# Storing the last output block by quarters, with its fourth quarter summed ahead of its second

## The chip, the cores and the metric

The kernel runs on one core of one Trainium2 chip. The metric is the device time of one execution in microseconds (us). Runs shown are medians of several executions; the profile comes from one execution of its own.

## What is computed

Hash attention over 4 x 8 heads (768 positions of 64 values each), whose output goes, as 3072 rows of 512 features, through a two-matrix block with a squared ReLU. In the reference, cut:

```python
q_bucket = ...   # 6 sign bits of q @ proj, as a number; k_bucket likewise
mask = q_bucket[:, :, :, None] == k_bucket[:, :, None, :]
scores = np.where(mask, scale * np.matmul(q, k.transpose(0, 1, 3, 2)), -1000000000.0)
...
attn = attn / (np.sum(attn, axis=-1, keepdims=True) + 1e-09)
x = np.matmul(attn, v)          # brought to (3072, 512)
h = x @ w_in                    # (512, 2048)
r = np.maximum(h, 0.0)
return ((r * r) @ w_out)        # (2048, 512), fp32
```

## The kernel before

The kernel has two stages. In the first, a loop over 16 pairs of heads hashes, scores, exponentiates and multiplies by the values, and leaves the attention output, feature by feature, in DRAM. In the second, a loop over three chunks of 1024 rows (`NCHUNK` = 3, `NCH` = 1024) computes the hidden layer and then calls `project(i)` for the second matrix.

Both matrices are multiplied by a fast scheme with seven half-size products in place of eight, applied twice for the second matrix: an outer round `k` of seven, and in each round seven inner products of 128 x 128 weight tiles (`leaf`) with 256 columns. The inner seven are written out in `product` (L828), in a fixed order: each of them adds four matmuls to one of three accumulators in PSUM (`add`, L837), ScalarE keeps running sums of them (`keep`, L844: `one`, `two`, `five`, `three`), and the four callbacks `c11`, `c12`, `c22`, `c21` take the four quarters out as soon as their operands are there. `c11`, `c12`, `c21` and `c22` are the quarters 0, 1, 2 and 3 of a block of 256 features x 512 rows: quarter `n` lies in row `n // 2` (128 features) and column `n % 2` (256 rows, `QN`). The work of every engine stands in the order of these calls; nothing is reordered later (`tc.manual_schedule()`).

The outer rounds add the quarters to sums that are kept in SBUF (`add_to`, L1196). A block of the output is finished in the second, sixth and fourth of the uses; the last round (`k` = 6) of the last chunk calls `fourth` and finishes the block `(ih, jh) = (1, 0)`, the last of the kernel. There `c11`, `c12` and `c22` each make two adds on VectorE (first a temporary from PSUM or from the kept sums, then the sum `o`), and `c21` makes one.

What stands in `o` has features on the partitions and must be turned. `close` does it when both quarters of a row are there:

- `put_out` (L1207): VectorE transposes the row's 128 x 512 in blocks of 32 x 32 (L1210), and four stores write it in pieces of 128 bytes (L1217). For the last block two of the four go through GpSimd's queue (POOL), two through SyncE's (SP).
- `put_last` (L1222), for the second row of the last block only: TensorE transposes each quarter in two 128 x 128 parts (L1227), ScalarE (quarter 3, L1232) or VectorE (quarter 2, L1234) copies the 128 x 256 from PSUM, and two stores on SP (quarter 3) or ScalarE's queue (quarter 2) write pieces of 512 bytes (L1237).

The buffers `h` that take what is to be stored are five (`NH`), used in turn, and each is free when its stores have landed.

Behind the last block every engine loads the flag `slow` (L1473) and branches on it (L1474): where it is set, a general version of the whole computation would run (`general`); here it is not, and the engines jump over that code. SyncE then waits for the semaphores of the DMAs, and all engines meet at a barrier (shown as L1671).

Of the kernel before, what the change touches and what calls it, by code (L numbers as in the profile page):

```python
# [8 lines left out]
FP32 = mybir.dt.float32  # L9
# [25 lines left out]
def kernel(  # L35
# [10 lines left out]
    nc = tc.nc  # L46
# [6 lines left out]
    P = 128  # L53
# [12 lines left out]
    NCH = 1024  # L66
    NCHUNK = B * S // NCH
# [3 lines left out]
    ident = glob.tile([P, P], FP32, name="ident")  # L71
# [10 lines left out]
    HF, HD, NR, NQ = DFF // 2, DM // 2, NFF // 2, NFF // 4  # L82
# [539 lines left out]
    for pr in range(NIN, NP):  # L622
        n = 16 if pr == NP - 1 else 1 + (pr % 3 == 0)
# [4 lines left out]
    def load_x(i, fs=slice(0, NFT)):  # L628

        if i not in xs:  # L630
            x = p_c.tile([P, NFT, NCH], FP32, name="x")
            xs[i] = x, [p_c.tile([P, 2, NCH // 2], FP32, name=f"t_x{n}") for n in range(3)]
        nc.gpsimd.dma_start(out=xs[i][0][:, fs], in_=x_all[:, fs, i * NCH:(i + 1) * NCH])
# [23 lines left out]
    with tc.manual_schedule():  # L657
# [158 lines left out]
        p_r = fast.enter_context(tc.tile_pool(name="p_r", bufs=2, reuse_waits="tile"))  # L816
        p_k = fast.enter_context(tc.tile_pool(name="p_k", bufs=1, reuse_waits="tile"))
        ps_m = fast.enter_context(tc.tile_pool(name="ps_m", bufs=2, space=PSUM, reuse_waits="tile"))
        HN, QN, NH = NCH // 2, NCH // 4, 5
# [5 lines left out]

        KEPT = dict(one=2, two=1, three=2, five=1)

        def product(n, w, at, bt, c11, c12, c21, c22, hook=None):  # L828

            acc = [ps_m.tile([P, 512], FP32, name=f"acc{i}")[:, 0:w] for i in range(3)]

            def add(to, a, b, first, last):
                for i in range(n):
                    nc.tensor.matmul(  # L837
                        out=acc[to], lhsT=a(i), rhs=b(i), start=first and i == 0,
                        stop=last and i == n - 1, skip_group_check=True,
                    )  # L840

            def keep(of, name):
                t = p_r.tile([P, 512], FP32, name=name, bufs=KEPT[name])[:, 0:w]
                nc.scalar.copy(out=t, in_=acc[of])  # L844
                return t

            add(0, at(0), bt["11"], True, False)
            one = keep(0, "one")
            add(1, at(1), bt["21"], True, True)
            if hook:  # L850
                hook()
            c11(acc[1], one)
            add(0, at(4), bt["t2"], False, False)
            two = keep(0, "two")
            add(2, at(3), bt["t1"], True, False)
            five = keep(2, "five")
            add(0, at(5), bt["t3"], False, False)
            three = keep(0, "three")
            add(2, at(6), bt["22"], False, True)
            c12(acc[2], two)  # L860
            c22(three, five)
            add(0, at(2), bt["t4"], False, True)
            c21(acc[0])

# [83 lines left out]
        def factor_units(n):  # L948

            src = [new_h().rearrange("p (a f c) -> p a f c", a=2, c=P) for _ in range(2)]  # L950
            for j in range(2):
                nc.gpsimd.dma_start(out=src[j], in_=w_in_7[j * NQ + n, :, 5:7])
            sums = [new_h().rearrange("p (a f c) -> p a f c", a=2, c=P) for _ in range(2)]
            sums_a(
                src[0][:, :, 0], src[0][:, :, 1], src[1][:, :, 0], src[1][:, :, 1],
                *(sums[j // 2][:, :, j % 2] for j in range(4)),
            )
            for m in range(2):
                nc.gpsimd.dma_start(out=w_in_49[n, :, 0:2, 2 * m:2 * m + 2], in_=sums[m])
# [246 lines left out]
        def put_out(i, ih, jh, n, o):  # L1206


            ot = p_r.tile([P, HN], FP32, name="h", bufs=NH)
            nc.vector.transpose(out=ot, in_=o)  # L1210
            m0 = ih * HD + n * P
            at = slice(i * NCH + jh * HN, i * NCH + (jh + 1) * HN)
            for a in range(P // 32):
                queue = nc.gpsimd if (ih, jh) == (1, 1) else nc.sync
                if (i, ih, jh) == (NCHUNK - 1, 1, 0) and a % 2:
                    queue = nc.gpsimd
                queue.dma_start(  # L1217
                    out=out[at, m0 + a * 32:m0 + (a + 1) * 32].rearrange("(c i) j -> i c j", i=32),
                    in_=ot[a * 32:(a + 1) * 32].rearrange("i (c j) -> i c j", j=32),
                )  # L1220

        def put_last(n, o):  # L1222

            row, col = n // 2, n % 2
            tp = ps_m.tile([P, 512], FP32, name=f"acc{col}")[:, 0:QN]
            for t in range(QN // P):
                nc.tensor.transpose(  # L1227
                    out=tp[:, t * P:(t + 1) * P], in_=o[:, t * P:(t + 1) * P], identity=ident
                )
            ot = p_r.tile([P, HN], FP32, name="h", bufs=NH)[:, 0:QN]  # L1230
            if col:
                nc.scalar.copy(out=ot, in_=tp)  # L1232
            else:
                nc.vector.tensor_copy(out=ot, in_=tp)  # L1234
            lo = (NCHUNK - 1) * NCH + col * QN
            for t in range(QN // P):
                (nc.sync if col else nc.scalar).dma_start(  # L1237
                    out=out[lo + t * P:lo + (t + 1) * P, HD + row * P:HD + (row + 1) * P],
                    in_=ot[:, t * P:(t + 1) * P],
                )  # L1240

        def project(i):
# [12 lines left out]
            def close(ih, jh, n):  # L1255
                o = outs[ih, jh, n // 2]
                o[1] += 1
                if (i, ih, jh, n // 2) == (NCHUNK - 1, 1, 0, 1):

                    if o[1] == 2:  # L1260
                        for col in (1, 0):
                            put_last(n - n % 2 + col, o[0][:, col * QN:(col + 1) * QN])
                elif o[1] == 2:
                    put_out(i, ih, jh, n // 2, o[0])

# [37 lines left out]
            for k in range(7):  # L1303
                b = OUTER[k][1]
                t1, t2 = tens.pop(k)
                if k == 0 and more:
                    load_x(i + 1)
                if i == 0 and 0 < k <= NQ:
                    factor_units(k - 1)
                if i == 0 and k == NQ + 1:  # L1310
                    load_peak(0)
                    load_peak(1)
                if k >= 5 and more:
                    load_inner(i + 1, 0, (k - 5,))
                at = lambda m, k=k: lambda n: leaves[k, m][:, n]
                bt = {
                    "11": lambda n: b[:, n, 0:QN], "21": lambda n: b[:, NQ + n, 0:QN],
                    "22": lambda n: b[:, NQ + n, QN:HN], "t1": lambda n: t1[:, n],
                    "t2": lambda n: t2[:, n], "t3": lambda n: b[:, n, QN:HN],
                    "t4": lambda n: b[:, NQ + n, 0:QN],  # L1320
                }

                def hook():
                    y21 = b[:, NQ:NR, 0:QN]
                    minus(y21, y21, t2)
                    if k + 1 < 7 and k not in (1, 3):
                        inner_sums(k + 1)
                    if k == 6 and more:
                        load_third_inner(i + 1, 0, nc.scalar)
                        sums_inner(i + 1)  # L1330

                counted = []

                def a_with_load(m, k=k):
                    load_leaf(7 * k + len(counted) + NLEAF - 2)
                    counted.append(m)
                    return at(m)

                use = uses[k]
                product(  # L1340
                    NQ, QN, a_with_load, bt, lambda *p: use(0, *p), lambda *p: use(1, *p),
                    lambda p: use(2, p, None), lambda *p: use(3, *p), hook,
                )
                if k in (3, 4) and i + 1 < NCHUNK:
                    sum_x(i + 1, 2 * k - 5)
                    sum_x(i + 1, 2 * k - 4)
                if k == 5 and i + 1 == NCHUNK:
                    guard()
                if k == 0:

                    for h in range(2):
                        at_h = slice(h * NQ, (h + 1) * NQ)
                        minus(b11[:, at_h], b22[:, at_h], b_t[:, at_h])
                    inner_sums(2)
                if k == 2:

                    for h in range(2):
                        at_h = slice(h * NQ, (h + 1) * NQ)
                        minus(b_t[:, at_h], b21[:, at_h], b11[:, at_h])
                    inner_sums(4)  # L1360
# [314 lines left out]
```

## Time and profile before

| | us |
|---|---|
| median of 3 runs (861.77 to 862.26) | 862.15 |
| time of the profiled execution | 861.97 |
| its span (first to last instruction) | 859.9 |
| TensorE busy | 848.5 |
| VectorE busy | 748.7 |
| ScalarE busy | 402.1 |
| GpSimd busy | 166.8 |

TensorE's granted clock is 0.998 over the span. The profile names the engines PE (TensorE), DVE (VectorE), ACT (ScalarE), POOL (GpSimd) and SP (SyncE); "SPq" and the like are instructions on an engine's queue that count as no busy time, such as the issue of a DMA. L1196 is line 1196 of the kernel. In the timeline each row has its start, its duration, and how many instructions it stands for; in the chain of waits each row is a piece of the chain of work that ended last.

### The profile page before, as it was taken

Reading aid. Unit: us, or ns where it says so; the run is one execution under the profiler, and the core shown is the slowest. Engines: PE = TensorE matmul, PEld = TensorE weight load, DVE = VectorE, ACT = ScalarE, POOL = GpSimd, SP = SyncE. Lnnn points to the kernel's source line nnn. Section 1 sums busy time; section 2 is a strip of 40 time slices with the busy share of each in tenths; the row PEclk is TensorE's granted clock in tenths of the full one; section 3 lists DMA queues with packets and bytes.
Section 4 is the critical chain, followed back from the end, with each engine's and each line's share of the span. In section 5 each row is a group of like instructions: output and inputs, shape, how many; then the busy total and the mean of one; then the engine's idle time right before and its main releaser. Section 6 shows DMA issues by size and latency. Waiting matters only on the chain.

```text
span 859.9 us, 16991 instructions
## 1 busy us (share of the span) xinstructions
PE 848.5 (99%) x6595; PEld 527.0 (61%) x6595; DVE 748.7 (87%) x1024; ACT 402.1 (47%) x752; POOL 166.8 (19%) x280
## 2 busy tenths in 40 slices
PE   8999999999999999999999999999999999999996
PEld 3544444444444444444788866657888765678885
DVE  5899999999999988988979978888889788888875
ACT  5887777888777752222111145553111355541110
POOL 1321111123221101642122121111000211100003
PEclk9999999999999999999999999999999999999999
DMA  9676889879998516999977975538558865345465
GB/s 204 133 149 150 179 176 203 208 162 252 250 229 209 179 58 237 337 320 300 349 234 220 265 191 192 186 110 299 164 151 201 195 203 179 122 129 159 148 177 107
DMA packets 234758, 170.14 MB, mean 198 GB/s; under 512 B 167944, under 2 KB 191824, under 8 KB 234672
## 3 DMA queue, kind: packets, MB, share of 16 engines
q1 hardware_dynamic: 194944, 87.85, 40.9%
q0 software_dynamic: 16480, 42.48, 15.8%
q10 hardware_dynamic: 23248, 38.68, 14.8%
q8 instruction: 53, 0.87, 0.4%
q14 instruction: 33, 0.27, 0.1%
HBM read 127.14 MB, written 41.16 MB: 196 GB/s over the span
## 4 chain that ended last, share of the span: by engine, by line
PE 98%; DVE 1%; DMA 1%; ACT 0%; issue 0%; DVEq 0%
PE acc L837 41%; PE st L430 18%; PE xo L485 14%; PE acc L1094 13%; PE acc L1047 8%; PE tot L534 2%; PE hash L360 1%; DMA qk_nat<-in_q_dram 1%; PE tp L320 0%; DVE bits L410 0%; ACT feat L327 0%; PE xo L360 0%; DVE o L1196 0%; ACT e L436 0%; PE acc L1227 0%
## 5 line engine op out<-in xcount | busy, mean ns | idle before, releaser
L436 ACT ACTIVATE e<-st 128x768 f32<-128x768 f32 x192 | 155.4, 810 | 58.3 <-PE st L430 55.3
L430 PE MATMUL st<-feat 64*64 64x384 f32 x1536 | 157.1, 483 | 1.0 <-DVE feat L329 1.0
L485 PE MATMUL xo<-e,v_nat 64*64 64x385 f32 (+1 forms) x1520 | 156.9, 483 | 0.0
L837 PE MATMUL acc<-b,leaf 128*128 128x256 f32 x600 | 133.2, 379 | 0.3 <-issue 0.3
L837 PEld LDWEIGHTS acc<-b,leaf 128*128 128x128 f32 x600 | 113.9, 190 | 16.6 <-issue 1.2
L473 DVE TENSOR_TENSOR total<-total,e 128x1536 f32<-128x1536 f32 x64 | 111.8, 1746 | 4.3 <-ACT e L436 2.8
L396 POOL DMA_DIRECT2D bits<-signed x120 | 61.9, 520 | 217.3 <-ACT signed L385 198.5
L485 PEld LDWEIGHTS xo<-e,v_nat 64*64 64x64 f32 (+1 forms) x1520 | 55.9, 133 | 67.9 <-issue 59.1
L1094 PE MATMUL acc<-t_x,w_unit 128*128 128x512 f32 x192 | 91.0, 596 | 0.0
L430 PEld LDWEIGHTS st<-feat 64*64 64x64 f32 x1536 | 55.7, 133 | 39.1 <-issue 33.5
L837 PE MATMUL acc<-t,leaf 128*128 128x256 f32 x336 | 75.9, 379 | 0.0
L837 PEld LDWEIGHTS acc<-t,leaf 128*128 128x128 f32 x336 | 63.8, 190 | 8.7
L909 DVE SCALAR_TENSOR_TENSOR b<-h 128x512 f32<-128x512 f32 x96 | 65.7, 691 | 3.0
L430 PE MATMUL st<-bits 64*64 64x384 bf16 x768 | 64.7, 325 | 0.1
L837 PE MATMUL acc<-x,w_unit 128*128 128x512 f32 x128 | 56.5, 593 | 0.0
L837 PE MATMUL acc<-b_t,leaf 128*128 128x256 f32 x240 | 53.8, 379 | 0.0
L844 ACT COPY two<-acc 128x256 f32<-128x256 f32 (+1 forms) x29 | 12.5, 431 | 87.5 <-PE acc L837 72.1
L1217 POOL DMA_DIRECT2D out_dram<-h x26 | 16.8, 654 | 186.0 <-DVE h L1210 184.4
L1094 PEld LDWEIGHTS acc<-t_x,w_unit 128*128 128x128 f32 x192 | 35.7, 190 | 27.0 <-issue 23.0
L837 PEld LDWEIGHTS acc<-b_t,leaf 128*128 128x128 f32 x240 | 45.5, 190 | 6.3
L844 ACT COPY one<-acc 128x256 f32<-128x256 f32 (+1 forms) x29 | 12.5, 431 | 78.7 <-PE acc L837 49.2
L430 PEld LDWEIGHTS <-bits 64*64 64x64 bf16 x768 | 23.8, 106 | 38.0 <-issue 37.1
(176 smaller groups left out, 1287.8 us busy)
## 6 DMA issues: line engine op xcount, KB each, us to landing
leaf<-w_out ACTq DMA_DIRECT2D x142, 256.0 KB, 3.1
raw<-in_moe_w_in_dram SPq DMA_DIRECT2D x8, 1024.0 KB, 6.7
raw<-in_moe_w_out_dram SPq DMA_DIRECT2D x8, 1024.0 KB, 7.6
w_unit<-w_in SPq DMA_DIRECT2D x16, 512.0 KB, 4.1
w_unit<-w_in SPq DMA_DIRECT2D x8, 896.0 KB, 8.3
w_out<-sums POOLq DMA_DIRECT2D x16, 448.0 KB, 8.0
v_nat<-in_v_dram SPq DMA_DIRECT2D x16, 384.0 KB, 5.2
x_all<-x_t SPq DMA_DIRECT2D x16, 384.0 KB, 3.1
```

The source lines that it names most:

```text
L396: nc.gpsimd.dma_start(out=t[h * D:h * D + NBITS + 1, w, c * HS:(c + 1) * HS], in_=signed[at:at + NBITS + 1, h],)
L430: nc.tensor.matmul(out=st[k * HK:(k + 1) * HK, h, 0:HS], lhsT=src[1][rows, key], rhs=src[0][rows, cut], start=first, stop=not first, skip_ ...
L436: nc.scalar.activation(out=key_of(pr, kt)[:, :, i, 0:HS], in_=st[:, :, 0:HS], func=ACTF.Exp, scale=scale)
L473: nc.vector.tensor_tensor(out=totals[pr], in0=totals[pr], in1=e, op=ALU.add)
L485: return nc.tensor.matmul(out=outs[pr][h * D:(h + 1) * D, c, 0:HS + 1], lhsT=nat[pr, "v_nat"][rows, h, kt * D:(kt + 1) * D], rhs=key_of(pr ...
L534: done = nc.tensor.matmul(out=spares[pr][g * 32:(g + 1) * 32, c2, 0:QS], lhsT=ones[rows], rhs=totals[pr][rows, h, c, c2 * QS:(c2 + 1) * QS ...
L837: nc.tensor.matmul(out=acc[to], lhsT=a(i), rhs=b(i), start=first and i == 0, stop=last and i == n - 1, skip_group_check=True,)
L844: nc.scalar.copy(out=t, in_=acc[of])
L909: nc.vector.scalar_tensor_tensor(out=out, in0=h, scalar=0.0, in1=h, op0=ALU.max, op1=ALU.mult)
L1047: nc.tensor.matmul(out=out, lhsT=w(a), rhs=b, start=start, stop=stop, skip_group_check=True)
L1094: nc.tensor.matmul(out=to, lhsT=w[:, PLACE[a], f], rhs=bt[b](f), start=first and f == 0, stop=last and f == NFT // 2 - 1, skip_group_check ...
L1217: queue.dma_start(out=out[at, m0 + a * 32:m0 + (a + 1) * 32].rearrange("(c i) j -> i c j", i=32), in_=ot[a * 32:(a + 1) * 32].rearrange("i ...
```

## The change

The order of the last two callbacks but one in `product` changes for the last round of the last chunk: quarter 3, which needs only the kept sums `three` and `five`, is taken ahead of quarter 1. Each quarter of the last block is turned and stored by itself as soon as it is summed. Quarters 0, 3 and 1 go through a 128 x 256 transpose on VectorE and four stores of 128-byte pieces each (`put_part`), two on SP and two on POOL. Quarter 2, the last, goes through TensorE in two parts, of which VectorE copies the first, which SP stores, and ScalarE copies and stores the second. Before, both quarters of the second row went through TensorE, and the first row was stored as a whole. The number of products, adds and copies of sums is the same; two 128 x 128 transposes on TensorE fall away, and three 128 x 256 transposes on VectorE stand for one of 128 x 512.

```diff
-        def product(n, w, at, bt, c11, c12, c21, c22, hook=None):
+        def product(n, w, at, bt, c11, c12, c21, c22, hook=None, last=False):
...
             add(2, at(6), bt["22"], False, True)
+            if last:
+                c22(three, five)
             c12(acc[2], two)
-            c22(three, five)
+            if not last:
+                c22(three, five)
             add(0, at(2), bt["t4"], False, True)
             c21(acc[0])
...
                 queue = nc.gpsimd if (ih, jh) == (1, 1) else nc.sync
-                if (i, ih, jh) == (NCHUNK - 1, 1, 0) and a % 2:
-                    queue = nc.gpsimd
...
+        LATE = {0: (nc.gpsimd, nc.sync), 3: (nc.sync, nc.gpsimd), 1: (nc.sync, nc.gpsimd)}
+
+        def put_part(n, o):
+
+            row, col = n // 2, n % 2
+            ot = p_r.tile([P, HN], FP32, name="h", bufs=NH)[:, 0:QN]
+            nc.vector.transpose(out=ot, in_=o)
+            lo = (NCHUNK - 1) * NCH + col * QN
+            m0 = HD + row * P
+            for a in range(P // 32):
+                LATE[n][a % 2].dma_start(
+                    out=out[lo:lo + QN, m0 + a * 32:m0 + (a + 1) * 32].rearrange(
+                        "(c i) j -> i c j", i=32
+                    ),
+                    in_=ot[a * 32:(a + 1) * 32].rearrange("i (c j) -> i c j", j=32),
+                )
+
         def put_last(n, o):
 
             row, col = n // 2, n % 2
-            tp = ps_m.tile([P, 512], FP32, name=f"acc{col}")[:, 0:QN]
-            for t in range(QN // P):
-                nc.tensor.transpose(
-                    out=tp[:, t * P:(t + 1) * P], in_=o[:, t * P:(t + 1) * P], identity=ident
-                )
             ot = p_r.tile([P, HN], FP32, name="h", bufs=NH)[:, 0:QN]
-            if col:
-                nc.scalar.copy(out=ot, in_=tp)
-            else:
-                nc.vector.tensor_copy(out=ot, in_=tp)
             lo = (NCHUNK - 1) * NCH + col * QN
             for t in range(QN // P):
-                (nc.sync if col else nc.scalar).dma_start(
+                at = slice(t * P, (t + 1) * P)
+                tp = ps_m.tile([P, 512], FP32, name=f"acc{t}")[:, 0:P]
+                nc.tensor.transpose(out=tp, in_=o[:, at], identity=ident)
+                if t:
+                    nc.scalar.copy(out=ot[:, at], in_=tp)
+                else:
+                    nc.vector.tensor_copy(out=ot[:, at], in_=tp)
+                (nc.scalar if t else nc.sync).dma_start(
                     out=out[lo + t * P:lo + (t + 1) * P, HD + row * P:HD + (row + 1) * P],
-                    in_=ot[:, t * P:(t + 1) * P],
+                    in_=ot[:, at],
                 )
...
-                if (i, ih, jh, n // 2) == (NCHUNK - 1, 1, 0, 1):
-
-                    if o[1] == 2:
-                        for col in (1, 0):
-                            put_last(n - n % 2 + col, o[0][:, col * QN:(col + 1) * QN])
+                if (i, ih, jh) == (NCHUNK - 1, 1, 0):
+                    put = put_last if n == 2 else put_part
+                    put(n, o[0][:, n % 2 * QN:(n % 2 + 1) * QN])
                 elif o[1] == 2:
                     put_out(i, ih, jh, n // 2, o[0])
...
                     lambda p: use(2, p, None), lambda *p: use(3, *p), hook,
+                    (i, k) == (NCHUNK - 1, 6),
```

## The prediction

> **What bounds the kernel now.** I read the page first (busy time and chain), then the chain of waits of the last 15 us, the timeline of VectorE and SyncE there, and the rows of the lines that end the program.
>
> ```profile
> span 859.9 us, 16991 instructions
> PE 848.5 (99%) x6595; PEld 527.0 (61%) x6595; DVE 748.7 (87%) x1024; ACT 402.1 (47%) x752; POOL 166.8 (19%) x280
> PE 98%; DVE 1%; DMA 1%; ACT 0%; issue 0%; DVEq 0%
> ```
>
> TensorE sets the pace for 851 of the 860 us. Its instructions up to the end of the last product are the same before and after (the built programs differ only in the transposes behind it), so only what follows that product can change. The chain there, in order of time:
>
> ```profile
> 844.84 4.55 PE acc L837 x21
> ...
> 849.48 0.44 DVE tmp L1196
> 849.92 0.02 issue
> 849.94 0.44 DVE o L1196
> 850.38 0.02 issue
> 850.40 0.71 DVE h L1210
> 851.11 0.32 DVE tmp L1196
> 851.43 0.02 issue
> 851.46 0.44 DVE o L1196
> 851.89 0.04 issue
> 851.94 0.78 PE acc L1227 x4
> 852.72 0.02 issue
> 852.74 0.42 DVE h L1234
> ```
>
> The chain leaves TensorE at 849.39, while TensorE works on: its last product runs to 851.10 (the timeline's last group of products starts at 845.76 and takes 5.34). So VectorE, not TensorE, is late: the add that needs the last product (L1196, `o<-sum,acc`) starts at 851.80, 0.7 us after its operand. The view ends with the last busy instruction, at 853.16; the span ends 6.7 us later. For these I read SyncE's rows. In the timeline, its last two stores:
>
> ```profile
> 852.81 0.84 SPq L1237 DMA_DIRECT2D out_dram<-h  x2
> ```
>
> Among the rows of the lines that end the program, the load of the flag, the branch on it and the waits behind it (duration in ns, first and last start):
>
> ```profile
> L1473 SPq TENSOR_LOAD <-slow x1: 735/735/735, 853.7 to 853.7; - x1
> ```
> ```profile
> L1474 SPq EVENT_SEMAPHORE  x8: 17/17/17, 857.7 to 858.2; - x8
> ...
> L1474 SPq COMPARE_BRANCH  x1: 50/50/50, 854.5 to 854.5; - x1
> ```
>
> And in the queue's own waits (us in total, times, longest):
>
> ```profile
> SPq L1474 <- SPq L1474: 3.1, 1, 3.1
> ```
>
> The reader is to see SyncE alone: two stores issued until 853.65, the flag loaded from 853.70, the branch at 854.51, then 3.1 us in which SyncE waits for nothing but itself, then its waits for the DMA semaphores from 857.66 and the final barrier to 859.9. The last store landed at 857.10 (issued by ScalarE at 853.61, 3.5 us), so the first of these waits came 0.55 us after everything had landed. The other engines had passed their branches by 855.3 and stood at the barrier (GpSimd's drain, 3.4 us, ended at 856.4). **The end is SyncE's own sequence behind its last store**, and what moves that store moves the end.
>
> **The change, part by part.** Times are of the profiled execution: span 859.9, its own time 861.97, 0.18 under the median 862.15.
>
> *Quarter 0, stored alone.* Its sum ends at 846.84 (846.42 + 0.43). VectorE then idled 2.64 us until 849.48. A 128x256 transpose is not in the trace; 128x384 takes 0.58 (L547), 128x512 0.71 (L1210), so 0.13 per 128 columns, and I take 0.45 (bounds: nothing, and 0.71). It lies in the idle time: 0. Its two SP and two POOL issues find free queues (POOL's earlier stores end at 847.45): 0.
>
> *Quarter 3 ahead of quarter 1.* It needs `three`, which ScalarE has ready at 848.06 (847.69 + 0.37). Add 0.38, add 0.42, transpose 0.45, and three gaps of 0.03: ready at 849.4, just before quarter 1's operand (849.48). With the transpose at 0.71 quarter 1 would start 0.25 late, but it has that much to spare: its two adds (0.44 each with their gaps) and a transpose end at 850.85, and the last product only comes at 851.10. So all this is hidden in VectorE's wait for TensorE; if the cover were gone, the chain would again carry the 1.2 us.
>
> *Quarter 2, the last.* Before, its add stood behind one 128x512 transpose (0.71) and quarter 3's two adds. Now it starts at 851.13 (851.10 and the 0.03 that ScalarE's copies lag behind TensorE), 0.67 earlier, and ends at 851.55. Then to SyncE's flag load:
> - add to transposes: 0.05 (852.22 to 852.27 before), so 851.60;
> - the first 128x128 transpose alone: 0.33 (L1227's longest) and 0.03, so the copy starts at 851.96;
> - VectorE copies 128x128. The rows are 0.42 for 128x256 (L1234) and 0.56 for 128x384 (L329): 0.29 by their slope. Bounds 0.18 (128x24, L555) and 0.42. I take 0.29, as it lies on the line of two PSUM copies: 852.25;
> - the issue starts 0.03 later, 852.28, and takes 0.35 to 0.44 (L1237): 0.40, to 852.68. There is one issue on SyncE instead of two;
> - the flag load begins 0.06 later: 852.74, against 853.70.
>
> Sum: **0.96 us earlier**, 0.8 to 1.1 with the bounds of copy and issue.
>
> *SyncE's queue.* Six issues of 128-byte pieces now stand ahead of the last store instead of two. Quarter 3's pair starts at 849.42, quarter 1's at 850.88. L1217 issues in this stretch took 0.32 to 0.91, median 0.49, so the queue is free at about 851.9, 0.4 before the last store: 0. If every one took 0.91, see below.
>
> *The other half on ScalarE.* Its transpose ends 0.11 after the first; a 128x128 copy is 0.27 (0.37 for 128x256, 0.59 for 128x512): issue at 852.37, against 853.20 and 853.61 before. With L1237's 3.5 to 3.8 us both last stores land by 856.2.
>
> *After the branch.* Branch at 853.55, 3.1 us, waits from 856.7, by which time the last store (856.2) has landed: 0.5 in hand, as before. The semaphores waited on are as many as before. GpSimd's last issue comes 0.26 earlier (851.79 against 852.05). So the whole 0.96 arrives at the end: 861.97 - 0.96 = 861.0, and on the median 862.15 - 0.96 = **861.2**.
>
> *The 3.1 us.* The trace shows an 8 KB instruction packet (q14) at 855.70 and another at 855.86, 1.2 us behind SyncE's branch, and no other engine waited more than 0.6 us at its branch. So I read the stall as a fetch of the branch's target, with a cost that starts at the branch and moves with it. [...] After the change SyncE has five instructions more ahead of the branch and jumps as far.
>
> **The rivals.**
> 1. *The stall is not a fixed cost* (the fetch is quicker, or the wait is really for the stores). Then the landing at 856.1 to 856.2 sets the end, without the 0.55 now lost: 857.66 - 856.1 = 1.55 earlier, 860.6. If the 0.55 goes with the landing, the end follows ScalarE's last issue, 853.61 to 852.37: 1.24 earlier, 860.9. For it: the stall is the largest piece behind the last product. Against it: SyncE was released well after the landing, and nothing shortens the jump.
> 2. *SyncE's queue becomes the bound, slower than before.* With all five issues from 849.42 on (quarters 3 and 1, and the last) at 0.91, the flag load starts at 849.42 + 5 x 0.91 + 0.06 = 854.03, 0.33 later than before: 862.5. It decides against the change from a mean of (853.64 - 849.42) / 5 = 0.84 per issue. The median 0.49 speaks against it; that the longest rows stand where DMA queues are full speaks for it.
> 3. *SyncE's code crosses a fetch boundary.* Its 26 instructions behind the branch now lie five further on. If they straddle a boundary of the 8 KB packets, a second stall of up to 3.1 us stands on the path: about 865. In the trace these packets follow SyncE's instruction count at a period of 128, and by this count 7 or so are left to the boundary.
> 4. *Nothing is gained*: the DMA traffic or the barrier, not SyncE, holds the end at 859.9: 862.1. Against it: every engine but SyncE has arrived by 856.4.
>
> **How the numbers follow.** Forecast 0.72 (861.2; 860.9 to 861.5 by itself), rival 1 0.13 (860.6 to 860.9), rival 2 0.07 (up to 862.5), rival 3 0.03 (865), rival 4 0.05 (862.1). The range 860.3 to 862.2 holds the forecast, rivals 1 and 4, and part of 2. About 0.2% (1.7 us) is what a measurement of this kernel can tell from no change; to be faster by that, the time must fall below 860.4, which is the far edge of rival 1 only: 0.06. Slower by that is rival 3: 0.03. Within: 0.91.
>
> **What would show it.** In the changed profile: no VectorE idle time ahead of quarter 3's add other than for `three`; the last add starting within 0.1 us of TensorE's last product; a 128x128 copy near 0.29; one SP store at about 852.3; SyncE's flag load near 852.7; again 3.1 us at its branch, and the span at about 858.9. I am wrong if SyncE's stall changes, if the flag load is not about 1 us earlier, or if a store lands after 856.7.

## The result, and the profile after

| | before | after |
|---|---|---|
| median of 20 runs (us) | 862.40 | 860.93 |
| ratio, 95% interval | | 0.9985 (0.9978 to 0.9992) |
| span of the profiled execution | 859.9 | 859.6 |
| end of TensorE's last product, from the span's start | 851.10 | 851.70 |
| from there to the span's end ("the tail") | 8.79 | 7.88 |

By the ratio the kernel is 1.3 us faster (0.7 to 1.9), against 0.96 forecast (861.2, counted from the 862.15 of three runs). The last product ended 0.6 us later in the second profile: what lies ahead of it scatters by more than the change is worth (849.9 to 853.3 in the profiles below). So from here on times are counted from the end of the last product, and the tail is what is compared: 0.9 us shorter.

The chain of the last microseconds, where before it left TensorE at 849.39:

```profile
845.87 5.84 PE acc L837 x27
851.72 0.02 issue
851.74 0.43 DVE o L1199
852.17 0.04 issue
852.21 0.45 PE acc L1248 x2
852.66 0.02 issue
852.69 0.27 ACT h L1250
```

It now stays on TensorE to the last product; one add, two transposes and a copy follow. VectorE's timeline shows the order that makes room (start, duration, instruction, idle time before it and what ended it):

```profile
847.48 0.45 DVE L1229 STREAM_TRANSPOSE h<-o 128x256 f32<-128x256 f32 x1
848.69 0.43 DVE L1199 TENSOR_TENSOR tmp<-three,five 128x256 f32<-128x256 f32 x1 [0.77 <-ACT three L844]
849.15 0.42 DVE L1199 TENSOR_TENSOR o<-sum,tmp 128x256 f32<-128x256 f32 x1
849.61 0.45 DVE L1229 STREAM_TRANSPOSE h<-o 128x256 f32<-128x256 f32 x1
850.01 0.42 DVE L1199 TENSOR_TENSOR tmp<-acc,two 128x256 f32<-128x256 f32 x1
850.47 0.42 DVE L1199 TENSOR_TENSOR o<-sum,tmp 128x256 f32<-128x256 f32 x1
850.93 0.45 DVE L1229 STREAM_TRANSPOSE h<-o 128x256 f32<-128x256 f32 x1
851.74 0.42 DVE L1199 TENSOR_TENSOR o<-sum,acc 128x256 f32<-128x256 f32 x1 [0.36 <-PE acc L837]
852.58 0.29 DVE L1252 COPY h<-acc 128x128 f32<-128x128 f32 x1 [0.42 <-PE acc L1248]
```

Of the 2.64 us that VectorE idled, 0.77 and 0.36 are left; where the last add once came 0.7 us late for TensorE's result, VectorE is now free 0.32 us before that result. SyncE's last rows answer to those of before: one store, the flag load, the branch and the first waits, and what it waited for in between.

```profile
852.90 0.35 SPq L1253 DMA_DIRECT2D out_dram<-h  x1
```
```profile
L1488 SPq TENSOR_LOAD <-slow x1: 516/516/516, 853.3 to 853.3; - x1
```
```profile
L1489 SPq EVENT_SEMAPHORE  x8: 17/17/17, 857.4 to 857.9; - x8
...
L1489 SPq COMPARE_BRANCH  x1: 50/50/50, 853.9 to 853.9; - x1
```
```profile
SPq L1489 <- SPq L1489: 3.4, 1, 3.4
```

Behind the last product: flag load at 1.60 (2.60 before), branch at 2.19 (3.40), next SyncE instruction at 5.65 (6.55). The stall behind the branch is still the largest piece.

### The profile page after: what moved, and what is told of

The parts are those of the page before. It is cut to its first block, busy times and chain, and to the rows that moved or that the text cites. A ratio compares the mean times of both kernels' runs of the same rounds, so it can differ in the third digit from the quotient of the medians.

```text
span 859.6 us, 17003 instructions
## 1 busy us (share of the span) xinstructions
PE 847.7 (99%) x6593; PEld 528.6 (62%) x6593; DVE 748.8 (87%) x1026; ACT 401.9 (47%) x752; POOL 169.0 (20%) x284
## 4 chain that ended last, share of the span: by engine, by line
PE 98%; DMA 1%; DVE 0%; ACT 0%; issue 0%; ACTq 0%; DVEq 0%
PE acc L837 41%; PE st L430 18%; PE xo L485 14%; PE acc L1097 13%; PE acc L1050 8%; PE tot L534 2%; PE hash L360 1%; DMA qk_nat<-in_k_dram 1%; ACT e L436 0%; DVE bits L410 0%; PE xo L360 0%; DVE feat L329 0%; PE tp L320 0%; ACTq L284 0%; PE acc L1248 0%
```

## The experiments

The theory is that of the prediction: the end is SyncE's own sequence behind its last store. The chief rivals are that the landing of the stores sets the end, and that one half of the change (the order, or the stores by quarters) makes the gain alone. Ratios are against the kernel before on the same chip, from 10 to 12 executions of the kernel in question (5 where the general version is left out; the padded kernel ran once and has no ratio). Times in the text are from the trace of one execution each, behind the last product.

### The order alone

Kernel before, with only the order changed:

```diff
+            if last:
+                c22(three, five)
             c12(acc[2], two)
-            c22(three, five)
+            if not last:
+                c22(three, five)
```

> Kernel before, with quarter 3 taken ahead of quarter 1 in the last round, and nothing else. The tail is the time from the end of TensorE's last product to the end of the span: 8.79 us before, 7.88 after the change. Theory (the end is SyncE's chain behind its last store): the last add starts at 0.04 behind the last product as after the change, but SyncE still waits for four transposes' first pair, a 128x256 copy (0.37) and two issues, so its flag load comes at 2.26 (2.60 before, 1.60 after): tail 8.45, a third of the gain. Rival (the order alone makes the gain): tail 7.9.

Ratio 1.0009 (1.0000 to 1.0018), tail 8.50. The last add came at 0.04, as expected. The flag load came at 1.90, earlier than I had worked out: quarter 3's transposes do not need the last add and followed the product directly. But SyncE's stall was 3.6, so that a flag load 0.7 earlier became a tail 0.3 shorter, and the time did not fall. Since time and tail disagreed, the same kernel ran again.

> e1_order_alone once more: its flag load came at 1.90 behind the last product (2.60 before, 1.60 after), its tail was 8.50, yet its time stood 0.1% over before (1.0000 to 1.0018). Theory (the end follows SyncE's flag load, and that time was what the rest of the program scattered): flag load at 1.90 again, tail 8.0 to 8.6, time 0 to 0.1% under before. Rival (the order alone costs something elsewhere): the time is over before again, with its interval above 1.

```profile
SPq L1478 <- SPq L1478: 4.0, 1, 4.0
```

Ratio 0.9998 (0.9986 to 1.0010); flag load at 1.98, stall 4.0, tail 9.01. The first run's hint of a cost is not confirmed, and the order alone gains nothing that can be measured: the stall took back what the flag load won. The last stores landed late as well, at 6.30 and 6.29 against 6.00 before, though they were issued 0.7 us earlier. That part of my theory, a stall that moves with the branch at a fixed length, fell here.

### The stores alone

Kernel after, with the order of before (the argument `last` always false).

> Kernel after, with quarter 1 ahead of quarter 3 as before; the stores by quarters stay. Theory: VectorE now has quarter 1's transpose, quarter 3's two adds and its transpose (0.45) between quarter 1's sum and the last add, which starts at 0.93 instead of 0.04; flag load at 2.48, tail 8.75: next to nothing of the gain is left. Rival (the stores by quarters make the gain whatever the order): tail 7.9.

VectorE's timeline at its end:

```profile
851.44 0.42 DVE L1199 TENSOR_TENSOR o<-sum,tmp 128x256 f32<-128x256 f32 x1
851.90 0.45 DVE L1229 STREAM_TRANSPOSE h<-o 128x256 f32<-128x256 f32 x1
852.27 0.38 DVE L1199 TENSOR_TENSOR tmp<-three,five 128x256 f32<-128x256 f32 x1
852.69 0.42 DVE L1199 TENSOR_TENSOR o<-sum,tmp 128x256 f32<-128x256 f32 x1
853.14 0.45 DVE L1229 STREAM_TRANSPOSE h<-o 128x256 f32<-128x256 f32 x1
853.51 0.38 DVE L1199 TENSOR_TENSOR o<-sum,acc 128x256 f32<-128x256 f32 x1
```

Ratio 1.0002 (0.9993 to 1.0011), tail 9.26. VectorE works without a gap up to the last add, 0.91 behind the product (which ended at 852.60): 0.93 was expected. Flag load at 2.44 (2.48 expected), stall 4.0 again. Neither half has the gain. The last store is issued at 1.82 with the order alone and at 2.12 with the stores alone, against 2.51 before and 1.28 with both: only together do they bring it forward by a microsecond.

### No general version to jump over

Kernel after, `general` reduced to one memset behind the flag, which leaves out the version of the computation for large inputs that these inputs never reach:

```diff
             const = inner.enter_context(tc.tile_pool(name="g_const", bufs=1))
-            w_out = const.tile([P, NFF, DM], FP32, name="g_w_out")
...
+            none = const.tile([D, NROW], FP32, name="none")
+            nc.vector.memset(none, 0.0)
```

> Kernel after, with the general version behind the flag left out (its body is one small memset, so that the branch jumps over a few instructions only); the flag is loaded and tested as before. Theory (SyncE's 3.1 to 3.4 us behind the branch are a fetch of the branch's target): the stall falls to about 0.5, SyncE then waits for the last landing (4.84 behind the last product) and the first wait ends there instead of at 5.65: tail 7.1. Rival (the wait behind the branch is for the stores, and comes 0.6 to 0.8 after the landing): tail 7.9 as after the change.

```profile
SPq L1518 <- DMA out_dram<-h: 0.3, 1, 0.3
```

Ratio 0.9945 (0.9931 to 0.9958), tail 4.38. The stall is gone (branch at 2.19, next instruction at 2.38), and SyncE's longest wait of that stretch for a store is the 0.3 above. The tail is 2.7 shorter than expected, mostly because the stores too landed sooner (the last at 3.06 instead of 4.84). SyncE also no longer has the eight waits of L1489, which took 0.6 us in the kernel after. In the rows of the last two stores (median and range from issue to landing), first this kernel, then the kernel after:

```profile
DMA to landing us min/median/max: 1.6/1.7/1.8
```
```profile
DMA to landing us min/median/max: 3.5/3.5/3.6
```

With the general version, one 16 KB and six 8 KB instruction packets moved from 853 to 860 us in the kernel after; here there were none. So about half of the 3.5 to 3.8 us that I had taken for a store's landing comes with the general version. That the packets hold up the stores is the reading that fits; it is not shown, since jumps and packets were only removed together.

The kernel before, with the general version left out in the same way:

> Kernel before, with the general version behind the flag left out, as e3_no_general has it for the kernel after. Without the fetches the stores landed 1.6 to 1.8 us after their issue there, and the span ended 1.32 behind the last landing. Theory: here the last store is issued at 2.51 and lands at 4.25, tail 5.6, so the change is worth 1.2 (the shift of the last issue) where nothing stands between landing and end, against 0.9 with the general version. Rival (the change gains by SyncE's branch alone): tail 4.4 as in e3_no_general.

Ratio 0.9961 (0.9948 to 0.9975), tail 6.33. The rival, that the change gains by SyncE's branch alone, falls: with no stall in either kernel the change is worth 1.95 in the tail (6.33 against 4.38, one profile each). The ratios differ by 0.0016, or 1.4 us, but their intervals overlap. My own 5.6 was missed too: the last stores landed 2.6 us after their issue, not 1.7. Their row:

```profile
DMA to landing us min/median/max: 2.6/2.6/2.8
```

The kernel before still has 128-byte pieces of its first row landing until 4.2 in this run, those after the change have all landed by 2.4. It also has four stores of 64 KB on the way at the end, where the kernel after has two. Either could be why its last stores take longer; this was not tried. The prediction had no term for it.

### SyncE done early

Kernel after, with what SyncE stored last moved to ScalarE's queue:

```diff
-        LATE = {..., 1: (nc.sync, nc.gpsimd)}
+        LATE = {..., 1: (nc.scalar, nc.gpsimd)}
...
-                (nc.scalar if t else nc.sync).dma_start(
-                    out=out[lo + t * P:lo + (t + 1) * P, HD + row * P:HD + (row + 1) * P],
-                    in_=ot[:, at],
-                )
+            nc.scalar.dma_start(
+                out=out[lo:lo + QN, HD + row * P:HD + (row + 1) * P].rearrange("(t p) m -> p t m", p=P),
+                in_=ot.rearrange("p (t m) -> p t m", m=P),
+            )
```

> Kernel after, with SyncE's last stores moved to ScalarE's queue: quarter 1's two, and quarter 2 as one store of both halves behind both copies. SyncE is done with quarter 3's stores, 0.8 us ahead of the last product's end, and its fetch runs beside the rest. Theory: branch near -0.1, fetched at 3.2, then the wait for the last landing (issue 1.3, landing 3.5 later, 4.8): tail 7.1. Rival (landing and a fixed time behind it set the end): tail 7.9; rival (ScalarE, whose flag load now comes last, stalls at its branch instead): tail 8 or more.

SyncE's rows:

```profile
L1491 SPq EVENT_SEMAPHORE  x8: 17/17/17, 854.2 to 856.5; - x8
L1491 SPq COMPARE_BRANCH  x1: 50/50/50, 851.3 to 851.3; - x1
```

Ratio 0.9973 (0.9964 to 0.9982), tail 6.91. The branch came at -0.19, the stall (2.9) ended at 2.74, and of the eight waits the fifth ended at 4.83, 0.01 behind the last landing (4.82). So once the stall lies beside other work, the landing sets the end. This kernel, the kernel after and the kernel before then ran once more, on one chip:

> e4_syncE_early once more, on the same chip as the kernel after. Theory: the end follows the last landing (4.8) whatever the stall, tail 6.9 within 0.3, and the time about 1 us under that of the kernel after.

> The kernel after, once more, for the spread of the tail (7.88 at the first profile; the stall behind SyncE's branch was 2.5 to 4.0 in the runs so far). Theory: flag load at 1.6 behind the last product again, tail 7.5 to 8.6 by the stall alone; the time 0.9 to 1.3 us under before.

> The kernel before, once more, for the spread of the tail (8.79). Theory: flag load at 2.6 again, tail 8.3 to 9.6 by the stall; the time within 0.1% of before, which shows what the timing can tell apart.

| | tail, two profiles | flag load | stall | ratio, first and second |
|---|---|---|---|---|
| before | 8.79, 8.92 | 2.60, 2.60 | 3.1, 3.3 | 1, 1.0000 (0.9990 to 1.0010) |
| after | 7.88, 7.68 | 1.60, 1.61 | 3.4, 3.2 | 0.9985, 0.9984 (0.9973 to 0.9995) |
| SyncE done early | 6.91, 7.11 | -0.75, -0.75 | 2.9, 2.6 | 0.9973, 0.9983 (0.9973 to 0.9992) |

The tails of these three repeat within 0.25 and the stalls within 0.3. The kernel with SyncE done early beats the kernel before in both runs; that it beats the kernel after shows in the tail (6.91 and 7.11 against 7.88 and 7.68). The ratios leave that open, since their intervals overlap both times; of the 1 us expected on the same chip, 0.5 was measured (medians of 860.84 and 861.35).

These repeats also tell the two chief causes apart. In eight profiles with SyncE's stall behind its last store (before and after twice each, the order alone twice, the stores alone, and the padded kernel below), the end came 2.23 or 2.24 us after SyncE's first instruction behind the stall, with tails from 7.7 to 9.3. From the last landing to the end it was anything from 2.2 to 3.2. So in these kernels SyncE's sequence sets the end. With SyncE done early it is the reverse: 2.09 us from the last landing to the end both times, and 4.2 and 4.6 from the stall.

### How far the jump goes

Kernel after, with the general version's loads and stores issued by GpSimd, so that in the built program SyncE jumps over 167 instructions instead of 270 and GpSimd over 222 instead of 140 (`nc.sync` to `nc.gpsimd` in `general`, 14 places).

> Kernel after, with the stores and loads of the general version (never run with these inputs) issued by GpSimd instead of SyncE; nothing that runs is changed. SyncE's branch then jumps over 167 instructions instead of 270, GpSimd's over 222 instead of 140. Theory (a jump stalls when it goes beyond the code already fetched): SyncE's stall falls to 0.5, GpSimd stalls instead, at 1.0 behind the last product and in time; SyncE waits for the last landing at 4.8: tail 7.1. Rival (every jump of this code stalls SyncE, however far): tail 7.9. Rival (GpSimd's stall comes onto the path, since it holds the barrier): over 7.9.

SyncE's waits, and the rows of GpSimd around its branch:

```profile
SPq L1686 <- DMA out_dram<-h: 2.3, 1, 2.3
...
SPq L1489 <- SPq L1489: 0.5, 1, 0.5
```
```profile
L1489 POOLq EVENT_SEMAPHORE  x4: 17/43/43, 855.0 to 855.2; - x4
...
L1489 POOLq COMPARE_BRANCH  x1: 58/58/58, 851.9 to 851.9; - x1
...
L1489 POOLq INC_SWDGE_SEM  x1: 707/707/707, 855.3 to 855.3; - x1
```

Ratio 0.9988 (0.9978 to 0.9997), tail 8.18 where 7.1 was expected. The stall went where the long jump went: SyncE's is 0.5, GpSimd's 3.0. Of the theory, the profile before shows SyncE's stall of 3.1 us behind its jump over 270 instructions and GpSimd's 0.5 behind its own over 140; that the distance decides was my estimate from these two, and what code has been fetched at a jump no run shows. The second rival came true as well: behind its stall GpSimd has waits of its own, a semaphore update of 0.7 and a drain of 2.2, which ended at 7.35 and now held the barrier. So the stall went with the long jump, and moving it to another engine is no gain.

The prediction's third rival, a second stall at a boundary of SyncE's code, was tried with 15 more instructions ahead of the branch:

```diff
+        pad = const.tile([P, 32], FP32, name="pad")
+        for j in range(30):
+            mark = nc.vector.memset(pad[:, j:j + 1], 0.0)
+            step = nc.sync.nop()
+            tc.add_manual_dep(step.ins, mark.ins.name, SYNC)
```

> Kernel after, with 30 one-element memsets on VectorE at the very start and waits for them on SyncE, which put 15 instructions more into SyncE's stream ahead of its branch (561 instead of 546). By the count of the 8 KB instruction packets (period 128), SyncE's 26 instructions behind the branch then straddle a boundary by about 8; after the change they end 7 short of it. Theory of rival 3 of the prediction: SyncE stalls a second time among its last waits, for the rest of a fetch that begins at its first wait: tail 7.9 + 1.7 = 9.6. Rival (both pages come with the jump, or the count is wrong): tail 7.9, with the one stall of 3 to 4 us.

Tail 7.69, one stall of 3.2 on SyncE, no second. The rival does not hold at this padding: either the following packet comes along with the jump, or my count of the boundary is off; which of the two stays open. The count is read off the trace before, where 8 KB packets started when SyncE had begun 82, 210, 339 (again at 340) and 465 of its instructions; the trace does not say which engine a packet is for. But the padding brought on a stall elsewhere. It puts 30 instructions more ahead of VectorE's branch, too, and VectorE's rows are now:

```profile
L1494 DVEq COMPARE_BRANCH  x1: 72/72/72, 852.9 to 852.9; - x1
...
L1494 DVEq EVENT_SEMAPHORE  x1: 21/21/21, 856.5 to 856.5; - x1
```

VectorE waited 3.6 us behind its branch, against 0.5 in every other kernel with the general version, and over the same code. It was back at 5.24, before SyncE (5.46), so that the tail shows nothing of it. The length of the jump is therefore not all: the same jump of VectorE's stalled when its branch stood 30 instructions further on. This is one profile.

### The last quarter on VectorE too

Kernel after, with `put_part` for all four quarters (quarter 2 by SyncE and ScalarE): TensorE transposes nothing.

> Kernel after, with quarter 2 also turned by VectorE's 32x32 blocks (0.45) and stored in 128-byte pieces, two stores on SyncE, two on ScalarE; TensorE transposes nothing. Theory: the first of the last stores is issued at 0.97 behind the last product instead of 1.20, but SyncE issues two of them (0.32 and 0.45) and loads its flag at 1.84 instead of 1.60: tail 8.1, 0.2 more than after the change, give or take the 0.5 by which the stall behind the branch differs between runs (2.9 to 4.0 so far). Rival (what the change gains at the last quarter is the larger pieces): the 128-byte pieces land later than 5.6 and the tail goes over 8.3 by that.

```profile
L1233 SPq DMA_DIRECT2D out_dram<-h x8: 315/429/1677, 848.0 to 853.7; - x8
```

Ratio 0.9993 (0.9984 to 1.0002), tail 7.98. The larger pieces are not the gain: the 128-byte pieces landed by 4.6. But one of SyncE's issues took 1.68 us, quarter 1's pair waited behind it, and the flag load came at 2.48 instead of 1.84. That is the prediction's second rival, in a kernel with eight issues. TensorE, which has no transposes left to issue, took its branch at -2.21, while its last products were still running, and a 16 KB instruction packet moved from -1.10 on, 1.1 us behind that branch and within the long issue; whether it was the cause was not tried. The stall was 2.5, the shortest of all, which is why the tail is near that of the kernel after.

## Why the prediction was right

Step by step, behind the last product (forecast from 851.10):

| step | forecast | measured |
|---|---|---|
| transpose 128x256 on VectorE | 0.45 | 0.45 |
| quarter 1 ready | -0.25 | -0.32 |
| last add starts | 0.03 | 0.04 |
| VectorE's copy of 128x128 | 0.29 | 0.29 |
| ScalarE's copy | 0.27 | 0.27 |
| SyncE's last issue starts, takes | 1.18, 0.40 | 1.20, 0.35 |
| flag load | 1.64 | 1.60 |
| branch | 2.45 | 2.19 |
| stall behind it | 3.1 | 3.4 |
| last store landed | 5.1 | 4.84 |
| tail | 7.83 | 7.88 |

The mechanism held at every step up to the flag load. Beyond it two terms were off and cancelled: the flag load took 0.52 instead of 0.74, and the stall 3.4 instead of 3.1. That the tail came within 0.05 us of the forecast is therefore partly luck. The stall's fixed length was the weak step, and one of the prediction's own signs of being wrong: over the runs the stall was 2.5 to 4.0, and it swallowed the gain in the kernel with the order alone.

The rivals: the first (the stall is no fixed cost) is true of the stall and did not change this result, since the kernel after had nearly the length of before (3.4 us against 3.1). Its other half, that the wait is really for the stores, does not hold: with SyncE done early the stall ended at 2.74, the last store landed at 4.82. The second (SyncE's issues) did not come: six issues took 0.32 to 0.47 (the longest before, 0.91, stood at 844.0, where the DMA engines were 0.99 busy from 843.4 to 845.6). It appeared in the all-VectorE kernel. The third was tried and did not show on SyncE; in that kernel VectorE stalled instead (3.6 us, against 0.5), with its code shifted by 30 instructions. The fourth (nothing gained) is excluded by the interval.

What the stall waits for is not shown. I read it as a fetch of the branch's target, from the 8 KB packets that moved within it: in the profile before they started 0.7, 1.2 and 1.4 us behind SyncE's branch, after the change 0.6, 0.9 and 1.2. Without the general version there was no packet there, and no stall. As to the length of the jump, the runs go with my estimate up to a point: the jumps over 270 instructions (SyncE) and 222 (GpSimd) stalled for 2.5 to 4.0 us, those over 167 (SyncE) and 140 (GpSimd, before and after) took 0.5, and VectorE's stalled for 3.6 us once 30 more instructions stood ahead of it.

What stays open: what sets the length of the stall (same kernel within 0.5, different kernels 2.5 to 4.0), why the last stores land later with the general version in place, and how much of the 1.3 us in time beyond the 0.9 to 1.2 in the tail is scatter of what lies ahead. The interval holds both.

## What to carry to other kernels

The chain of busy work ends before the program does (here, after the change, at 852.96 of 859.6 us): read on, in the queue's own rows, to the last store, the branch and the barrier, and ask which engine arrives last there. Where two edits each take a different piece of work off one engine's last stretch, neither need show alone, so test them together before dropping either. Compare a change at the end of a long kernel from its last common event on; the ratio of whole times hardly resolves a microsecond in 860.

## What the runs showed of the hardware

- The long jumps (SyncE's over 270 instructions, GpSimd's over 222) cost 2.5 to 4.0 us from the branch to the engine's next instruction. VectorE's jump cost 0.5 us, and 3.6 us in the one kernel that had 30 more instructions ahead of it.
- A block of code that never runs, at the end of this kernel, cost it 3.5 us (tail 7.88 to 4.38; ratio 0.9985 to 0.9945). Without it the last stores landed in 1.7 us instead of 3.5.
- 128-byte pieces were no bar to an early landing: SyncE's stores of 32 KB in 128-byte pieces took 1.5 to 2.8 us after the change, its 64 KB in 512-byte pieces, which were issued later, 3.5. Without the general version SyncE's last two of the former took 1.8 and 2.1 us, the latter 1.6. So these runs rank neither.
- One issue on SyncE's queue took 1.68 us, against 0.43 in the median of the eight in that kernel.
